# Holding the weight splits of one round in issue order, loading a quarter unit later, and moving one logits block's split

## The chip, the cores and the metric

The kernel runs on one core of a Trainium2 chip. The metric is device time in microseconds of one execution; the kernel before took 1881.35 us, the median of 3 runs (1880.4 to 1882.02).

## The reference

The computation is an attention step with 32 packed queries, a feed-forward layer with squared ReLU, and a mixture of 8 experts whose gates are balanced in 8 alternating steps over rows and columns. B = 4, H = 8, S = 576, so N = 2304 tokens of D = 512.

```python
def _moe_ref(x, w_in, w_out) -> np.ndarray:
    h = np.maximum(x @ w_in, 0.0)
    return (h * h @ w_out).astype(np.float32)
...
    logits = x @ w_gate
    logits = logits - logits.max()
    P = np.exp(logits)
    for _ in range(8):
        P /= P.sum(1, keepdims=True) + 1e-09
        P /= P.sum(0, keepdims=True) + 1e-09
        P *= N / E
    out = np.zeros((N, D), dtype=np.float32)
    for e in range(E):
        h = np.maximum(x @ w1[e], 0.0)
        ye = h @ w2[e]
        out += P[:, e:e + 1] * ye
```

## The kernel before

Every fp32 operand of a matmul is split into a hi and a lo half in float32r, and a product is three matmuls (hi·hi, hi·lo, lo·hi). The first expert layer, x @ w1, runs as seven block products by a Strassen-like scheme: w1 is taken as A11, A12, A22 and the sums S1 to S4, x as B11, B21, B22 and T1 to T4.

The tokens go through the experts in three groups. The first, 512 tokens (two halves of 256), is the "512-token round": from 426.8 to about 790 us of the span, before which the kernel does attention and the feed-forward layer, and after which the two other groups follow from kept, already split weights. The round has NQ = 32 units (a quarter of an expert's 1024 hidden columns each, some 11 us). `unit(n, ...)` issues the seven products into three PSUM banks X, Z and Y (line 679: 128x256 matmuls, six a product), the copies of partial sums (`s`, ACT, lines 740, 748, 751), the adds (VectorE: line 742 the first Y add, 755 the Z add, 758 the second Y add), and after each a ReLU into a hi half (ACT, line 686) and a lo half (VectorE, line 687) of h. Between products it issues one y unit, the matmuls of an older unit's h with w2 (line 709, 128x512). After products A12, S2, S3 and A22 it calls `hook(n, i, at)` for quarter i = 0 to 3.

A hook does the weights' work: `split_w` takes the next blocks of the table `splits` (a unit has two of w2 and four of w1). One split is a hi half on ACT (line 160), a lo half on GpSimd (line 161) and for w1 a store of both to DRAM on SP's queue. w1's block 0 also issues four sums on VectorE into one tile `wt` (lines 137 to 140), which blocks 1 and 2 are split from. When a raw tile has given its last split, `load_w` issues the next load (512 KB, ACT's queue, line 109). In this round two of every four raw tiles come from a pool `rx` whose space was used by earlier pools, `cvt` (tags cc, cr, cx) and `bdp0` of `ab` among them.

The hook then does what the table `extra` names, such as logits, and in units 2 to 7 one step of `balance`: `rows_step` (VectorE, lines 639 to 644: sums of rows rs, their reciprocal, the product P, column sums cs) or `cols_step` (a matmul on cs, line 649, and lines 651 to 653).

The order on each engine comes from a scheduler that may move instructions ahead of others. For n > 0 `extra` and the balancing stand inside `pinned()`, which makes what is issued in it come after the last instruction so far of every engine; the splits stand outside it.

`logits_split(k, ...)` splits block k of the second layer's input x2 into four tiles lx (ACT line 447, GpSimd line 448) and `logits(k, ...)` multiplies them with the gate weights (line 455), copies the result (line 458), transposes it (line 462) and copies it into P (line 463). Block 7's four tiles lie in `bdp0` and in the three tags of `cvt`; block 8's in four tiles of tag h2 in `pb`.

Of the kernel before, what the change touches and what calls it, by code (L numbers as in the profile page):

```python
# [11 lines left out]
F32R = mybir.dt.float32r  # L12
# [12 lines left out]
BT = 2 * S // 3  # L25
# [12 lines left out]
def kernel(ctx: ExitStack, tc: tile.TileContext, qT, kT, v, pT,  # L38
# [3 lines left out]
    @contextmanager  # L42
    def pinned():

        traced = nc.cur_bb.bb.instructions
        with ExitStack() as st:
            for engine in {i.engine for i in traced[-400:]}:
                st.enter_context(tc.issue_after(next(i for i in reversed(traced) if i.engine == engine)))
            yield

    def open_pool(name, **kw):
        st = ExitStack()
        return st, st.enter_context(tc.tile_pool(name=name, bufs=1, reuse_waits="tile", **kw))

    def pool(name, **kw):
        st, p = open_pool(name, **kw)
        ctx.push(st)
        return p
# [8 lines left out]
    stAB, ab = open_pool("ab", side="right")  # L67
# [26 lines left out]
    STEPS = ("A11", "S1", "S4", "S2", "S3", "A12", "A22")  # L94
    W, raw = {}, {}
    wpools = [wpa, None, None]
    state = {"load": 0, "split": 0}

    def load_w():
        k = state["load"]  # L100
        if k >= len(loads):
            return
        state["load"] += 1
        kind, src = loads[k]
        more = state.get("more")
        where = stage if more is None or (k - more[0]) % 4 >= 2 else more[1]
        t = where.tile([128, 512], I64, tag="raw", name="raw64", bufs=2) if kind == "f64" else \
            where.tile([128, 1024], F32, tag="raw", name="raw", bufs=2)
        (nc.sync if more is None else nc.scalar).dma_start(t, src)
        raw[k] = t  # L110

    def from_f64(t):

        v = t.bitcast(I32).rearrange("p (n two) -> p n two", two=2)
        high, low = v[:, :, 1].bitcast(F32), v[:, :, 0].bitcast(U32)
        a = cvt.tile([128, 512], F32, tag="cx", name="ca")
        c = cvt.tile([128, 512], I32, tag="cc", name="cc")  # L120
        r = cvt.tile([128, 512], I32, tag="cr", name="cr")
        nc.scalar.activation(a, high, AF.Copy, scale=2.0 ** -112)
        nc.vector.tensor_scalar(c, a.bitcast(I32), 3, None, op0=ALU.logical_shift_left)
        nc.scalar.activation(r, low, AF.Copy, scale=2.0 ** -29)
        nc.vector.scalar_tensor_tensor(c, a.bitcast(I32), -0x80000000, c, op0=ALU.bitwise_and, op1=ALU.bitwise_or)
        nc.gpsimd.tensor_tensor(c, c, r, op=ALU.add)
        return c.bitcast(F32)
# [16 lines left out]
    def split_w(n=1):  # L144
        for _ in range(n):
            k = state["split"]
            if k >= len(splits):
                return
            state["split"] += 1
            key, l, i = splits[k]  # L150
            part = k % 12 >= 8
            w = wpools[part].tile([128, 2, 512], F32R, tag="w", name="w", bufs=4 if part else 8)
            if loads[l][0] == "f64":
                t = from_f64(raw[l])
            elif key[0] == "w2":
                t = raw[l][:, i * 512:(i + 1) * 512]
            else:
                t = w1_blocks(raw[l], i)
            n = t.shape[1]
            nc.scalar.activation(w[:, 0, :n], t, AF.Copy)  # L160
            nc.gpsimd.tensor_tensor(w[:, 1, :n], t, w[:, 0, :n].bitcast(F32), op=ALU.subtract)  # L161
            W[key] = w
            if key[0] == "w1":
                there = kept.tile([128, 2, 512], F32R, name=f"kept_w1_{key[1]}_{i}")
                nc.sync.dma_start(there[:, :, :n].bitcast(F32), w[:, :, :n].bitcast(F32))
                KEPT[key[1], i] = there, n
            if k + 1 == len(splits) or splits[k + 1][1] != l:
                load_w()


    AT = [(ta if b < 2 else ab).tile([128, 2, 2, S], F32R, tag=f"at{b}", name=f"at{b}", bufs=1) for b in range(B)]
# [145 lines left out]
    def bank(kind):  # L317
        r = banks[kind]
        p, tag, bufs = r[turn[kind] % len(r)]
        turn[kind] += 1  # L320
        return p.tile([128, 512], F32, tag=tag, name="ps" + kind, bufs=bufs)
# [3 lines left out]
    def gslot(f, b, g):  # L325

        if f == 0:
            return b // 2, b % 2
        if f == 1:
            return ((1, 0), (0, 0))[g] if b < 2 else (3 - b, 1)  # L330
        return (1, g) if b < 2 else (0, b - 2)
# [3 lines left out]
    def g_unit(f, bp, j):  # L335

        ps = bank("h")
        w = W["win", f, j]
        st = BDP[bp]
        for i, (x, y) in enumerate(((0, 0), (0, 1), (1, 0))):  # L340
            nc.tensor.matmul(ps, st[:, x, j, :], w[:, y, :], start=(i == 0), stop=(i == 2))  # L341
        for bb in range(2):
            b = 2 * bp + bb
            if j % 2 == 0:
                side, n = gslot(f, b, j // 2)
                gt[b] = gpools[side].tile([128, 2, 512], F32R, tag=f"g{n}", name="g", bufs=2)
                G[f, b, j // 2] = gt[b]
            r = ((j % 2) ^ bb) * 64
            hi, lo = gt[b][r:r + 64, 0, :], gt[b][r:r + 64, 1, :]
            nc.scalar.activation(hi, ps[r:r + 64, :], AF.Copy)  # L350
            nc.vector.tensor_tensor(lo, ps[r:r + 64, :], hi.bitcast(F32), op=ALU.subtract)

    HT, HB1 = {}, 6
# [87 lines left out]
    def logits_split(k, places):  # L441
        p = next(q for q in (2, 1, 0) if GROUPS[q][0] <= 256 * k)
        o = 256 * k - GROUPS[p][0]
        for kd, (where, tag) in enumerate(places):
            t = where.tile([128, 2, 256], F32R, tag=tag, name="lx", bufs=HB1 if tag == "h2" else 1)
            src = X2[p][:, kd, o:o + 256]
            nc.scalar.activation(t[:, 0, :], src, AF.Copy)
            nc.gpsimd.tensor_tensor(t[:, 1, :], src, t[:, 0, :].bitcast(F32), op=ALU.subtract)
            LG[k, kd] = t
# [58 lines left out]
    stPB, pb = open_pool("pb", side="right")  # L508
# [51 lines left out]
    for i, (f, c) in enumerate(seq):  # L560
        if i < 3:
            continue
        k = c + len(THIRDS) - len(BLOCKS[f])
        last = f == NFC - 1
        if k < 2 and f > 0:
            for j in (2 * k, 2 * k + 1):
                g_unit(f, 1, j)
        if last and k == 0:
            nc.sync.dma_start(wgr, wg)
            nc.gpsimd.memset(wgs.bitcast(F32), 0.0)  # L570
            nc.scalar.activation(wgs[:, :, 0:E], wgr, AF.Copy)
            nc.vector.tensor_tensor(wgs[:, :, E:2 * E], wgr, wgs[:, :, 0:E].bitcast(F32), op=ALU.subtract)
        moe1(i, [lambda: logits_step(*MIDDLE[k])] if last and k in MIDDLE else (), 2 if i == 3 else 0)
        if last:
            logits_step(*END[k])
        if last and k == 2:
            stG.close()
            xca = pool("xca", side="left")
            T0 = {i: xca.tile([128, 4, 2, GROUPS[0][1]], F32R, tag=f"x{i}", name="xc0", bufs=1) for i in (0, 2)}
            operand(0, "B11", (T0[0][:, 0], T0[0][:, 1]), nc.gpsimd)  # L580
            operand(0, "B21", (T0[0][:, 2], T0[0][:, 3]), nc.gpsimd)
            operand(0, "B22", (T0[2][:, 0], T0[2][:, 1]), nc.gpsimd)
        if last and k == 3:
            for i in (1, 3):
                T0[i] = ta.tile([128, 4, 2, GROUPS[0][1]], F32R, tag=f"at{i // 2}", name="xc0", bufs=1)
            operand(0, "T1", (T0[1][:, 0], T0[1][:, 1]), nc.vector)
            operand(0, "T2", (T0[1][:, 2], T0[1][:, 3]), nc.vector)
        if last and k == 4:
            operand(0, "T3", (T0[2][:, 2], T0[2][:, 3]), nc.vector)
            x21, x22 = x_block(0, 1, 0), x_block(0, 1, 1)  # L590
            nc.vector.tensor_tensor(x21, x21, x22, op=ALU.subtract)
        split_w({2: 3, 3: 3, 4: 2}.get(k, 0))
        if k in (3, 4) and f + 1 < NFC:
            for j in (2 * (k - 3), 2 * (k - 3) + 1):
                g_unit(f + 1, 0, j)
    logits_split(8, ((pb, "h2"),) * 4)
    stPB.close()
    stCV.close()
# [222 lines left out]
        extra[22 + 2 * k, 3] = lambda k=k, name=name: operand(2, name, xc_tile(2, *SLOT[name]), (nc.gpsimd, nc.vector)[k % 2])  # L821

    def hook(n, i, at):
        split_w((2, 2, 1, 1)[i])
        if n == 0:
            extra.get((n, i), lambda: None)()
            return
        with pinned():
            extra.get((n, i), lambda: None)()
            if n > 2 and i != 1 or (n, i) == (2, 3):  # L830
                balance()
# [322 lines left out]
```

## Time and profile before

| what | us |
| --- | --- |
| median of 3 runs | 1881.35 |
| lowest, highest | 1880.4, 1882.02 |
| the profiled execution itself | 1880.53 |
| its span | 1878.7 |
| TensorE busy | 1854.2 |
| VectorE, GpSimd, ACT busy | 1275.1, 1047.3, 832.5 |

The profiled execution is 0.8 us below the median. PE is TensorE, DVE is VectorE, POOL is GpSimd, SP is the engine whose queue holds the stores. The page gives busy time by engine and the chain of work that ended last; windows cut the span into stages; waits say which instruction of another engine ended an engine's idle time; a timeline lists one engine's instructions in order of time.

### The profile page before, as it was taken

To read this page: it belongs to the slowest core of one execution; us is meant where nothing else is said; L and a number is where in the kernel's file an instruction comes from. 1 tells how busy PE (TensorE), PEld (TensorE's weight loads), DVE (VectorE), ACT (ScalarE), POOL (GpSimd) and SP (SyncE) were. 2 spreads that over 40 slices of the span, in tenths; PEclk is the share of its full clock that TensorE was granted. 3 is DMA by queue.
4 is the path that set the end of the run, shared out by engine and by line. 5 is a ranking of instruction groups with operands and counts; after the bars stand their busy time and mean duration, and the time that the engine had idled before them with its cause. 6 is when DMAs were issued, how large, how long until landed. Compare 5 with 4: busy or idle time off the path is not lost.

```text
span 1878.7 us, 28608 instructions
## 1 busy us (share of the span) xinstructions
PE 1854.2 (99%) x10244; PEld 1687.8 (90%) x10244; DVE 1275.1 (68%) x2095; ACT 832.5 (44%) x1557; POOL 1047.3 (56%) x655
## 2 busy tenths in 40 slices
PE   8999999999999999999999999999999999999998
PEld 7899999998888898888888888888889999999998
DVE  5767676744755556478877887788775666666665
ACT  6667554544465455444434343343334232332323
POOL 3214221436667677367877877777774444444444
PEclk9999999999999999999999999999999999999999
DMA  7402210206788877677777677676788777777874
GB/s 283 160 25 89 68 45 24 102 1 221 251 271 309 303 267 274 211 231 245 241 239 254 223 252 253 229 247 231 241 293 289 261 263 265 259 262 247 265 252 146
DMA packets 153821, 403.55 MB, mean 215 GB/s; under 512 B 14232, under 2 KB 65360, under 8 KB 153680
## 3 DMA queue, kind: packets, MB, share of 16 engines
q1 hardware_dynamic: 118928, 345.10, 54.0%
q10 hardware_dynamic: 34752, 56.63, 9.8%
q8 instruction: 81, 1.33, 0.3%
q14 instruction: 60, 0.49, 0.1%
HBM read 273.96 MB, written 127.72 MB: 214 GB/s over the span
## 4 chain that ended last, share of the span: by engine, by line
PE 93%; DVE 3%; ACT 1%; POOL 1%; DMA 1%; issue 1%; ACTq 0%; DVEq 0%; POOLq 0%
PE psc L679 35%; PE psx L1044 16%; PE psz L1044 12%; PE psy L399 11%; PE psy L709 8%; PE psh L380 6%; PE psh L341 1%; PE pp L247 1%; PE s L281 1%; POOL w L161 1%; PE s L215 0%; ACT w L160 0%; PE psy L455 0%; DVE wt L139 0%; DMA raw<-w 0%
## 5 line engine op out<-in xcount | busy, mean ns | idle before, releaser
L679 PE MATMUL psc<-xc,w 128*128 128x256 f32 (+2 forms) x4032 | 778.2, 336 | 3.0 <-ACT s L740 1.2
L679 PEld LDWEIGHTS psc<-xc,w 128*128 128x128 f32 x4032 | 666.2, 188 | 69.2 <-DVE psc L758 1.6
L1020 POOL TENSOR_TENSOR hh<-hb,hh 128x1024 fp32r<-128x1024 f32 (+1 forms) x224 | 504.4, 2256 | 372.4 <-ACT hh L1019 298.2
L1019 ACT ACTIVATE hh<-hb 128x1024 fp32r<-128x1024 f32 (+1 forms) x224 | 213.9, 955 | 448.3 <-DVE hb L1017 194.7
L1044 PE MATMUL psx<-hh,wa 128*128 128x512 f32 (+1 forms) x1536 | 352.7, 362 | 0.0
L1044 PEld LDWEIGHTS psx<-hh,wa 128*128 128x128 f32 x1536 | 278.9, 188 | 30.1 <-ACT hh L1019 0.4
L1044 PE MATMUL psz<-hh,wa 128*128 128x512 f32 (+1 forms) x1152 | 261.8, 362 | 0.3 <-issue 0.3
L1044 PEld LDWEIGHTS psz<-hh,wa 128*128 128x128 f32 x1152 | 209.1, 188 | 22.8 <-issue 0.6
L161 POOL TENSOR_TENSOR w<-raw,w 128x512 fp32r<-128x512 f32 (+1 forms) x128 | 156.6, 1237 | 124.5 <-ACT w L160 111.8
L399 PE MATMUL psy<-h,w 128*128 128x384 f32 (+1 forms) x1200 | 222.3, 330 | 0.3 <-ACT x L405 0.3
L709 PE MATMUL psy<-w,hh 128*128 128x512 f32 x768 | 202.9, 396 | 4.6 <-ACT hh L686 3.6
L399 PEld LDWEIGHTS psy<-h,w 128*128 128x128 f32 x1200 | 200.7, 188 | 0.9 <-ACT x L405 0.5
L1052 DVE TENSOR_TENSOR acc<-psx,acc 128x512 f32<-128x512 f32 (+1 forms) x248 | 151.9, 617 | 70.6 <-PE psx L1044 69.5
L1052 DVE TENSOR_TENSOR acc<-psz,acc 128x512 f32<-128x512 f32 (+1 forms) x184 | 112.6, 619 | 93.0 <-PE psz L1044 93.0
L950 DVE SCALAR_TENSOR_TENSOR hb<-psc,gate 128x512 f32<-128x512 f32 (+1 forms) x256 | 157.2, 619 | 12.2 <-PE psc L679 7.3
L709 PEld LDWEIGHTS psy<-w,hh 128*128 128x128 f32 x768 | 135.3, 189 | 29.6 <-ACT hh L686 5.3
L924 POOL TENSOR_TENSOR wa<-rb,wa 128x512 fp32r<-128x512 f32 x80 | 132.6, 1666 | 41.1 <-ACT wa L923 30.7
L1017 DVE TENSOR_TENSOR hb<-hb 128x1024 f32<-128x1024 f32 (+1 forms) x96 | 133.1, 1387 | 28.8 <-POOL hh L1020 27.9
L380 PE MATMUL psh<-at,g 128*128 128x384 f32 (+2 forms) x768 | 127.2, 304 | 0.0
L380 PEld LDWEIGHTS psh<-at,g 128*128 128x128 f32 x768 | 114.2, 189 | 1.7
L161 POOL TENSOR_TENSOR w<-cc,w 128x512 fp32r<-128x512 f32 x32 | 42.1, 1315 | 107.7 <-ACT w L160 72.5
L161 POOL TENSOR_TENSOR w<-wt,w 128x512 fp32r<-128x512 f32 x64 | 83.3, 1313 | 19.9 <-ACT w L160 15.1
(144 smaller groups left out, 1862.1 us busy)
## 6 DMA issues: line engine op xcount, KB each, us to landing
w<-kept_w SPq DMA_DIRECT2D x184, 512.0 KB, 4.4
kept_w<-wa SPq DMA_DIRECT2D x112, 512.0 KB, 4.3
wa<-kept_w SPq DMA_DIRECT2D x112, 512.0 KB, 4.5
kept_w<-w SPq DMA_DIRECT2D x96, 512.0 KB, 4.8
raw<-w ACTq DMA_DIRECT2D x60, 512.0 KB, 5.8
rb<-w ACTq DMA_DIRECT2D x64, 256.0 KB, 4.4
w<-kept_w SPq DMA_DIRECT2D x61, 256.0 KB, 4.0
raw<-win SPq DMA_DIRECT2D x16, 512.0 KB, 3.9
```

The lines of the kernel that those rows point to most:

```text
L161: nc.gpsimd.tensor_tensor(w[:, 1, :n], t, w[:, 0, :n].bitcast(F32), op=ALU.subtract)
L380: nc.tensor.matmul(ps[:, u - begin:w - begin], gw[:, x, m * 128:(m + 1) * 128], at[:, y, g, u - b * S:w - b * S], start=(i == 0), stop=(i ...
L399: nc.tensor.matmul(ps[:, :n], w[:, x, d * 128:(d + 1) * 128], h[:, y, :], start=(i == 0), stop=(i == 11))
L679: last = nc.tensor.matmul(ps[:, :N], w[:, u, o + k * 128:o + (k + 1) * 128], x[v][:, k, :], start=(start and k + u + v == 0), stop=(k == 1 ...
L709: nc.tensor.matmul(ps, h[:, x, o:o + 128], w[:, y, :], start=(n % 4 + m + x + y == 0), stop=(n % 4 == 3 and m == 1 and x == 1), skip_group ...
L924: nc.gpsimd.tensor_tensor(w[:, 1], src, w[:, 0].bitcast(F32), op=ALU.subtract)
L950: nc.vector.scalar_tensor_tensor(HB[q][m, t][:, nn, :], src, 0.0, GATE[p, g // 4][:, t * N:(t + 1) * N], op0=ALU.max, op1=ALU.mult)
L1017: nc.vector.tensor_tensor(src, src, hb[MINUS[k]], op=ALU.subtract)
L1019: nc.scalar.activation(hi, src, AF.Copy)
L1020: nc.gpsimd.tensor_tensor(lo, src, hi.bitcast(F32), op=ALU.subtract)
L1044: nc.tensor.matmul(ps, A2[q, k][:, u, nn, d * 128:(d + 1) * 128], OPS[7 * q + k][v][:, nn, :], start=(first and nn + u + v == 0), stop=(nn ...
L1052: nc.vector.tensor_tensor(a, ps, a, op=ALU.add)
```

## The change

It has three parts. In the round, the call of `split_w` moves inside `pinned()`, so that from unit 1 on a quarter's splits (ACT, GpSimd, VectorE's sums and SP's stores) come after the last instruction issued before them on each engine. The load that a finished raw tile sets off is no longer issued at once but counted in `state["due"]` and issued at the start of the next hook. And block 7's split lies in one tile of nine rows, in the space of `at3`, in place of the four tiles in `bdp0` and `cvt`; tiles that nobody uses turn the rotation of h2 so that block 8's split takes other slots. Line numbers behind the diff's places shift by up to 15 (679 becomes 691, 686 becomes 698, 687 becomes 699, 709 becomes 721, 742 becomes 754, 755 becomes 767, 758 becomes 770).

```diff
--- before.py
+++ after.py
@@ -94,7 +94,7 @@
     STEPS = ("A11", "S1", "S4", "S2", "S3", "A12", "A22")
     W, raw = {}, {}
     wpools = [wpa, None, None]
-    state = {"load": 0, "split": 0}
+    state = {"load": 0, "split": 0, "due": 0}
 
     def load_w():
         k = state["load"]
@@ -165,7 +165,14 @@
                 nc.sync.dma_start(there[:, :, :n].bitcast(F32), w[:, :, :n].bitcast(F32))
                 KEPT[key[1], i] = there, n
             if k + 1 == len(splits) or splits[k + 1][1] != l:
-                load_w()
+                state["due"] += 1
+            if "more" not in state:
+                load_due()
+
+    def load_due():
+        while state["due"]:
+            state["due"] -= 1
+            load_w()
 
 
     AT = [(ta if b < 2 else ab).tile([128, 2, 2, S], F32R, tag=f"at{b}", name=f"at{b}", bufs=1) for b in range(B)]
@@ -441,8 +448,11 @@
     def logits_split(k, places):
         p = next(q for q in (2, 1, 0) if GROUPS[q][0] <= 256 * k)
         o = 256 * k - GROUPS[p][0]
+        if k == 7:
+            whole = ab.tile([128, 9, 256], F32R, tag="at3", name="lx7", bufs=1)
         for kd, (where, tag) in enumerate(places):
-            t = where.tile([128, 2, 256], F32R, tag=tag, name="lx", bufs=HB1 if tag == "h2" else 1)
+            t = whole[:, 1 + 2 * kd:3 + 2 * kd, :] if k == 7 else \
+                where.tile([128, 2, 256], F32R, tag=tag, name="lx", bufs=HB1 if tag == "h2" else 1)
             src = X2[p][:, kd, o:o + 256]
             nc.scalar.activation(t[:, 0, :], src, AF.Copy)
             nc.gpsimd.tensor_tensor(t[:, 1, :], src, t[:, 0, :].bitcast(F32), op=ALU.subtract)
@@ -593,6 +603,8 @@
         if k in (3, 4) and f + 1 < NFC:
             for j in (2 * (k - 3), 2 * (k - 3) + 1):
                 g_unit(f + 1, 0, j)
+    for _ in range(-len(HT) % HB1):
+        pb.tile([128, 2, BT], F32R, tag="h2", name="unused", bufs=HB1)
     logits_split(8, ((pb, "h2"),) * 4)
     stPB.close()
     stCV.close()
@@ -821,11 +833,14 @@
         extra[22 + 2 * k, 3] = lambda k=k, name=name: operand(2, name, xc_tile(2, *SLOT[name]), (nc.gpsimd, nc.vector)[k % 2])
 
     def hook(n, i, at):
-        split_w((2, 2, 1, 1)[i])
         if n == 0:
+            load_due()
+            split_w((2, 2, 1, 1)[i])
             extra.get((n, i), lambda: None)()
             return
         with pinned():
+            load_due()
+            split_w((2, 2, 1, 1)[i])
             extra.get((n, i), lambda: None)()
             if n > 2 and i != 1 or (n, i) == (2, 3):
                 balance()
```

The order of TensorE in unit 0, around the logits of block 7 (lx, lx7: the split x2; psc: a product's bank; w_4777: a half of w2). Before:

```order
L679 MATMUL psc_4757<-xc0_4419,w_4246 128x256 x6
L455 MATMUL psy_4816<-lx_4698,wgs_1354 128x256 x2
L455 MATMUL psy_4816<-lx_4701,wgs_1354 128x256 x2
L455 MATMUL psy_4816<-lx_4704,wgs_1354 128x256 x2
L455 MATMUL psy_4816<-lx_4707,wgs_1354 128x256
L679 MATMUL psc_4756<-xc0_4419,w_4246 128x256 x6
L679 MATMUL psc_4757<-xc0_4229,w_4251 128x256 x6
L709 MATMUL psy_5010<-w_4777,hh_4774 128x512 x2
L709 MATMUL psy_5038<-w_4777,hh_4774 128x512 x2
L679 MATMUL psc_4756<-xc0_4229,w_4251 128x256 x6
L709 MATMUL psy_5010<-w_4777,hh_4774 128x512
L709 MATMUL psy_5038<-w_4777,hh_4774 128x512
L455 MATMUL psy_4816<-lx_4707,wgs_1354 128x256
```

Now:

```order
L691 MATMUL psc_4756<-xc0_4419,w_4246 128x256 x6
L465 MATMUL psy_4815<-lx7_4698,wgs_1354 128x256 x8
L691 MATMUL psc_4755<-xc0_4419,w_4246 128x256 x6
L472 MATMUL psy_4826<-both_1355,lgT_4824 128x8 x2
L691 MATMUL psc_4756<-xc0_4229,w_4251 128x256 x6
L721 MATMUL psy_5007<-w_4776,hh_4773 128x512 x2
L721 MATMUL psy_5035<-w_4776,hh_4773 128x512 x2
L721 MATMUL psy_5007<-w_4776,hh_4773 128x512
L721 MATMUL psy_5035<-w_4776,hh_4773 128x512
```

All eight matmuls on the split stand together, where the eighth stood behind two products and six y matmuls.

The order of ACT from the end of unit 0 into unit 1 (P: the gate copy; raw: a weight as loaded; psc_4887 and psc_4884: bank X of unit 1). Before:

```order
L686 ACTIVATE hh_4877<-psc_4756 128x256
L463 ACTIVATE P_1357<-psy_4827 128x16
L109 DMA raw_4752<-w2 128x1024
L109 DMA raw_4754<-w1 128x1024
L463 ACTIVATE P_1357<-psy_4867 128x16
L160 ACTIVATE w_4908<-raw_4752 128x512
L160 ACTIVATE w_4911<-raw_4752 128x512
L740 ACTIVATE s_4890<-psc_4887 128x256
L748 ACTIVATE s_4916<-psc_4888 128x256
```

Now:

```order
L109 DMA raw_4751<-w2 128x1024
L109 DMA raw_4753<-w1 128x1024
L698 ACTIVATE hh_4876<-psc_4755 128x256
L473 ACTIVATE P_1357<-psy_4866 128x16
L752 ACTIVATE s_4887<-psc_4884 128x256
L698 ACTIVATE hh_4902<-psc_4886 128x256
L109 DMA raw_4905<-w1 128x1024
L160 ACTIVATE w_4907<-raw_4751 128x512
L160 ACTIVATE w_4910<-raw_4751 128x512
L760 ACTIVATE s_4913<-psc_4885 128x256
```

Two loads that stood behind the gate copy stand ahead of it, and the s copy of unit 1 stands ahead of the two splits of w2 that read the first of them, not behind.

The order of VectorE in unit 3, from the lo half of h to the second Y add. Before:

```order
L687 SCALAR_TENSOR_TENSOR hh_5179<-psc_5163,hh_5179 128x256
L639 TENSOR_REDUCE rs_5196<-P_1357 128x18
L640 TENSOR_SCALAR rs_5196<-rs_5196 128x18
L641 RECIPROCAL rs_5196<-rs_5196 128x18
L137 TENSOR_TENSOR wt_5364<-raw_5147 128x256
L139 TENSOR_TENSOR wt_5364<-raw_5147 128x256
L642 TENSOR_TENSOR P_1357<-P_1357,rs_5196 128x144
L138 TENSOR_TENSOR wt_5364<-wt_5364,raw_5147 128x256
L755 TENSOR_TENSOR psc_5162<-psc_5162,s_5211 128x256
L644 TENSOR_REDUCE cs_5201<-P_1357 128x8
L140 TENSOR_TENSOR wt_5364<-raw_5147,wt_5364 128x256
L758 TENSOR_TENSOR psc_5163<-psc_5161,s_5203 128x256
```

Now:

```order
L699 SCALAR_TENSOR_TENSOR hh_5176<-psc_5160,hh_5176 128x256
L651 TENSOR_REDUCE rs_5193<-P_1357 128x18
L652 TENSOR_SCALAR rs_5193<-rs_5193 128x18
L653 RECIPROCAL rs_5193<-rs_5193 128x18
L654 TENSOR_TENSOR P_1357<-P_1357,rs_5193 128x144
L656 TENSOR_REDUCE cs_5198<-P_1357 128x8
L137 TENSOR_TENSOR wt_5219<-raw_5042 128x256
L139 TENSOR_TENSOR wt_5219<-raw_5042 128x256
L138 TENSOR_TENSOR wt_5219<-wt_5219,raw_5042 128x256
L767 TENSOR_TENSOR psc_5159<-psc_5159,s_5208 128x256
L140 TENSOR_TENSOR wt_5219<-raw_5042,wt_5219 128x256
L770 TENSOR_TENSOR psc_5160<-psc_5158,s_5200 128x256
```

The row step now stands in one piece ahead of the four sums of wt, which were mixed with it, and three of the sums stand ahead of the Z add in either order. On ACT and GpSimd the two splits of unit 3's own w2 have moved too: before they stood ahead of the unit's first s copy, now they stand behind its first hi half of h, with one split of w1 behind them.

## Rows read from the trace of the kernel before

**Rows 1.** The page: busy time of the engines, and the chain that ended last, by engine

```profile
PE 1854.2 (99%) x10244; PEld 1687.8 (90%) x10244; DVE 1275.1 (68%) x2095; ACT 832.5 (44%) x1557; POOL 1047.3 (56%) x655
...
PE 93%; DVE 3%; ACT 1%; POOL 1%; DMA 1%; issue 1%; ACTq 0%; DVEq 0%; POOLq 0%
```

**Rows 2.** Windows by stage: length, busy time (x instructions), granted clock, DMA share, GB/s

```profile
426.80:441.18 14.38, 14.13 (x93) 12.29 (x91) 4.28 (x10) 5.41 (x15) 8.39 (x9) 1.00 0.71 231
441.18:454.15 12.97, 10.62 (x63) 8.46 (x62) 8.78 (x14) 6.60 (x16) 9.28 (x9) 1.00 0.54 189
454.15:543.28 89.13, 85.25 (x525) 74.38 (x525) 62.88 (x154) 48.02 (x111) 57.07 (x47) 1.00 0.74 255
543.28:785.20 241.92, 239.66 (x1491) 213.47 (x1489) 130.73 (x264) 126.85 (x297) 168.82 (x132) 1.00 0.83 285
785.20:805.00 19.80, 19.17 (x84) 15.24 (x84) 15.62 (x23) 6.41 (x11) 1.29 (x1) 1.00 0.50 170
sum 378.20, PE 368.84 PEld 323.84 DVE 222.30 ACT 193.28 POOL 244.85; mean PE 73.77 PEld 64.77 DVE 44.46 ACT 38.66 POOL 48.97
```

**Rows 3.** TensorE's waits, 426.8 to 805 us: total us, times, longest

```profile
PE psy L709 <- ACT hh L686: 3.6, 6, 0.8
PE psy L649 <- DVE cs L644: 2.2, 4, 0.6
```

**Rows 4.** TensorE's timeline: start, us, line, operation, [idle before <-releaser]

```profile
429.00 0.99 PE L455 MATMUL psy<-lx,wgs 128*128 128x256 f32 x7
...
433.89 0.28 PE L455 MATMUL psy<-lx,wgs 128*128 128x256 f32 x1
...
473.60 0.39 PE L649 MATMUL psy<-cs,ones 128*128 128x8 f32 x2 [0.53 <-DVE cs L644]
```

**Rows 5.** ACT's timeline, unit 1

```profile
437.77 0.82 ACTq L109 DMA_DIRECT2D raw<-w  x2
...
443.09 1.15 ACT L160 ACTIVATE w<-raw 128x512 fp32r<-128x512 f32 x2 [1.62 <-DMA raw<-w]
```

**Rows 6.** VectorE's timeline, unit 1

```profile
444.40 0.95 DVE L137 TENSOR_TENSOR wt<-raw 128x256 f32<-128x256 f32 x1 [5.08 <-DMA raw<-w]
```

**Rows 7.** GpSimd's timeline, unit 0

```profile
431.78 1.45 POOL L448 TENSOR_TENSOR lx<-x,lx 128x256 fp32r<-128x256 f32 x2
```

**Rows 8.** TensorE's timeline, unit 3: its first four products

```profile
467.14 3.11 PE L679 MATMUL psc<-xc,w 128*128 128x256 f32 x24
```

**Rows 9.** VectorE's timeline, unit 3

```profile
469.81 0.42 DVE L687 SCALAR_TENSOR_TENSOR hh<-psc,hh 128x256 fp32r<-128x256 f32 x1 [0.45 <-ACT hh L686]
...
470.47 0.41 DVE L640 TENSOR_SCALAR rs<-rs 128x18 f32<-128x18 f32 x1
...
472.26 0.30 DVE L642 TENSOR_TENSOR P<-P,rs 128x144 f32<-128x144 f32 x1
...
473.47 0.41 DVE L140 TENSOR_TENSOR wt<-raw,wt 128x256 f32<-128x256 f32 x1
...
476.85 1.23 DVE L640 TENSOR_SCALAR rs<-rs 128x18 f32<-128x18 f32 x1
...
478.41 1.05 DVE L642 TENSOR_TENSOR P<-P,rs 128x144 f32<-128x144 f32 x1
```

**Rows 10.** GpSimd's timeline, unit 3

```profile
476.75 1.30 POOL L161 TENSOR_TENSOR w<-raw,w 128x512 fp32r<-128x512 f32 x1 [1.20 <-ACT w L160]
478.01 1.29 POOL L161 TENSOR_TENSOR w<-wt,w 128x512 fp32r<-128x512 f32 x1
```

**Rows 11.** Groups of VectorE and GpSimd, 426.8 to 785 us: busy us, mean ns

```profile
L139 DVE TENSOR_TENSOR wt<-raw 128x256 f32<-128x256 f32 x29 | 22.6, 781 | 0.0
...
L642 DVE TENSOR_TENSOR P<-P,rs 128x144 f32<-128x144 f32 x8 | 5.5, 688 | 0.1
L161 POOL TENSOR_TENSOR w<-raw,w 128x512 fp32r<-128x512 f32 x94 | 129.4, 1390 | 80.2 <-ACT w L160 68.8 <-DMA kept_w<-w 6.7 <-PE psc L679 4.1
```

**Rows 12.** The page's DMA issues: KB each, median us to landing

```profile
raw<-w ACTq DMA_DIRECT2D x60, 512.0 KB, 5.8
```

## The prediction

> **What bounds the kernel now.** I read the page first: TensorE is busy for 1854.2 us of a span of 1878.7 and has 93% of the chain that ended last [rows 1]. So nothing can be won except TensorE's idle time, about 24 us in all, and anything that makes TensorE wait longer is paid in full. The granted clock is 1.00 in each stretch of the round [rows 2], so no price here is one of the clock.
>
> Next the windows by stage: the round that the change touches runs from 426.8 to 805 us and holds 378.20 - 368.84 = 9.4 us of that idle time (the sum of the stretches [rows 2]). A stretch's length less TensorE's busy time says where it lies: 0.25 in unit 0, 12.97 - 10.62 = 2.35 in unit 1, 89.13 - 85.25 = 3.9 in units 2 to 7 with the balancing, 2.3 from unit 8 on (0.5 of it just ahead of 785.2) and 0.6 in the passage to the next round. Ahead of 421 us the order of every engine is unchanged, and behind the round only some loads of later weights are issued a few places apart, some 40 us ahead of their first use. So the change can win 9.4 us at most, 0.5% of the run. What a measurement of this kernel can tell from no change is about 0.2%, which is 3.8 us.
>
> Then the waits that end TensorE's idle time in the round: most are ended by ACT's evacuations of h (3.6 us in 6 waits, the longest 0.8) and VectorE's column sums of the balancing (cs: 2.2 in 4) [rows 3]. The timeline puts the four for cs, of which one stands in [rows 4], into units 3 to 5; with four of 0.3 to 0.65 for h they make up the 3.9 of units 2 to 7. Unit 1 has one wait for ACT's s copy and two for h.
>
> **Units 0 and 1: the wait for raw goes.** ACT issued the first two loads into the new raw tiles at 437.77, behind a gate copy that ends the logits of block 7, since the tiles lie on the space of that block's split x2. ACT then stood idle for the load until 443.09, with two splits of w2, which read it, next in its queue and the s copy of unit 1 behind them [rows 5], and VectorE stood 5.08 us on the same load, with the first sum of wt ahead of the Y add [rows 6]. TensorE's three waits in unit 1, 2.35 us, follow from this. In the new order the loads stand before the gate copy, and s and hh stand ahead of the first split that needs a load, so I take off all of it: **-2.35**.
>
> **Unit 0: a new wait.** Before, TensorE did seven of the eight matmuls of logits 7 at 429.00 and the eighth at 433.89, behind other work [rows 4]. Now all eight stand together ahead of the S2 product. The eighth needs the last lo half of the split x2, which stands in GpSimd's order where it stood, behind three splits from raw and one from wt: it starts at 431.78, and a pair takes 1.45, so the first of the two is done at 432.5 [rows 7]. TensorE has done seven by 429.9 and waits 2.6; the 0.25 at 430.25 lies inside that. **+2.35**: the two terms cancel.
>
> **Units 2 to 7: the balancing meets the splits.** Now each quarter unit's splits are held behind that quarter's evacuation, and the balancing steps behind these. I walk unit 3, from its first product (467.14 in the trace); in the trace the lo half of h ends 3.1 us in [rows 8, 9].
>
> What decides is what VectorE's operations on SBUF cost beside GpSimd. In the trace the scalar add on rs took 0.41 alone and 1.23 when GpSimd's split ran from 476.75 to 478.05; the product P took 0.30 alone and 1.05 when one ran from 478.01 to 479.30. Each ended within 0.2 us of that split's end [rows 9, 10]. So they waited for the running split. The sums of wt show the same: the 29 of L139 average 0.78, where 0.41 is one alone [rows 9, 11].
>
> With that cost in full: rs ends 3.4 us in, the splits of w2 run on GpSimd from 3.3 to 4.6 and to 5.9 and the next one to 7.2 (1.3 each [rows 10]). The scalar add ends at 4.6, the reciprocal at 4.9, P at 6.0, cs at 6.45. The first sum of wt waits until 7.2 and ends at 7.4; two more sums, the Z add, the fourth sum and the Y add follow at about 0.34 each, to 9.1. TensorE: four products end at 2.95 [rows 8], the first y matmuls wait 0.3 for w2's hi half and take 0.7, S4 and S3 (1.43) end at 5.4, the matmul on cs waits 1.0, four y matmuls end at 7.5, and A22, which accumulates onto what the Y add reads, waits 1.6. That is **2.9** with the rest, where before had 0.53. If instead no operation waits for GpSimd (0.41, 0.30, sums 0.41), cs is there at 4.75 and the Y add is done at 6.9, where A22 could start at 6.5: **0.7**. The same walk by the long prices gives 0.9, 2.9, 2.3, 1.05, 1.35 and 2.9 for units 2 to 7, 11.4 together; by the short ones I put 2.0 for the six. Against today's 3.9 the term lies between **-1.9 and +7.5**. In the trace about half of these operations are lengthened (a mean of 0.78 between 0.41 and some 1.2); now GpSimd's three splits stand back to back exactly where rows_step runs, which is nearer the long end, so I take two thirds of the way: **+4.4**.
>
> The Trainium skill's page "SBUF — State Buffer", section "SBUF: two separate sides", says that a VectorE operation with two SBUF inputs and a GpSimd one that reads SBUF exclude each other for a whole instruction. The trace agrees for P (1.05 beside a split, 0.30 alone). By that rule every one of them would wait, the term would be +7.5 and the time about 1889.
>
> **Units 8 to 31.** No balancing runs here. By the same walk the Z and Y adds keep 1 to 2 us ahead of the product that needs them, and the last w2 half arrives before its y matmuls. The 2.3 - 0.5 = 1.8 of this stretch may go or stay, and as many as four waits of the longest kind for h (0.8 [rows 3]) may come: -1.8 to +3, and I take **0**. The loads start a quarter unit later, 2.8 us of 11; a raw tile is then read about a unit after its issue, and a load has landed in 5.8 [rows 12], so this costs nothing; a load slower than some 10 us would be the end of that cover. The two unused h2 tiles and one tile in place of four add no work.
>
> **Sum.** 1880.53 (the profiled execution) - 2.35 + 2.35 + 4.4 + 0 = 1884.9. The median of the runs is 0.8 above the profiled one: **1885.7**, 0.23% over 1881.35.
>
> **The rivals.**
> *Faster.* VectorE's balancing and sums find gaps between GpSimd's splits. Then units 2 to 7 take their short end (-1.9), and with order on ACT the lone waits for h go as well (-1.8); if also half of the wait for the eighth logits matmul is covered because GpSimd reaches the last lo half sooner (-1.2), the time is 1881.35 - 4.9 = 1876.4. It turns on GpSimd: GpSimd has gaps (80 us of idle time ahead of its splits of raw, most of it ended by ACT's hi halves [rows 11]), and a sum that falls into such a gap costs 0.41. Against it: three of GpSimd's six splits of a unit need no sum and stand ahead of the first. It decides for faster if fewer than about one in five of these operations is lengthened. Chance 0.16.
> *No change.* The gain at units 0 and 1 and the cs waits are given back by the eighth matmul and a third of the contention: -1.9 + 0.33 x 9.4 = +1.2, so 1882.5; without any contention, but with today's lone waits, 1879.5. This also holds the case in which the held order does little because the dependencies had set it already. For it: the total at stake is small, and half the contended operations are paid now. Chance 0.40.
> *Slower*, the forecast, 1885.2 to 1892 (long end +7.5 and +3). Chance 0.44.
>
> **How the numbers follow.** Slower by over 0.2% is over 1885.1, faster is under 1877.6. The range takes in the no-change case whole, the near edge of the faster one, and the forecast up to its long end of 1889: 1877 to 1890; outside lie some 0.12 below and 0.06 above. The slower case's own range is 1885 to 1890.
>
> **What would show it.** Right: TensorE no longer waits for s at unit 1's start, and ACT's split waits for raw no more; a wait of some 2.6 us before the eighth logits matmul near 430, ended by GpSimd; in units 3, 4 and 7 waits of TensorE ended by VectorE's cs or Y add; P and the scalar add on rs near 1 us in most steps (P's mean is now 0.69 [rows 11]). Wrong: if P and the sums fall towards 0.4, the faster rival holds; if waits for cs stay and none for the Y add appears, no change; if w waits for raw in later units, my cover for the later loads was wrong.

## The result, and the profile after

The changed kernel takes 1894.55 us (median of 4 runs, 1894.45 to 1897.33) against 1881.03 for the kernel before, measured beside it: a ratio of 1.0075, 95% interval 1.0057 to 1.0092. It is slower by 13.5 us, in the direction forecast and three times as far. The profiled execution has a span of 1892.7 us, 14.0 more than before.

The page of the changed kernel, the two parts that answer to [rows 1]:

```profile
PE 1858.3 (98%) x10244; PEld 1689.8 (89%) x10244; DVE 1313.7 (69%) x2095; ACT 831.3 (44%) x1557; POOL 1052.8 (56%) x655
...
PE 91%; DVE 5%; ACT 1%; issue 1%; POOL 1%; DMA 0%; ACTq 0%; POOLq 0%; DVEq 0%
PE psc L691 35%; PE psx L1059 16%; PE psz L1059 12%; PE psy L406 11%; PE psy L721 8%; PE psh L387 6%; PE psh L348 1%; PE pp L254 1%; PE s L288 1%; DVE wt L137 1%; DVE wt L139 1%; DVE wt L138 1%; PE s L222 0%; POOL w L161 0%; PE psy L465 0%
```

TensorE is busy 4.1 us longer with the same instructions, so its idle time has grown by 9.9, not 14.0; VectorE is busy 38.6 us longer (1313.7 - 1275.1), also with the same instructions, and the sums of wt (lines 137 to 139) are now in the chain. Both need an explanation that the order of the instructions alone doesn't give.

Windows by stage, to be held against [rows 2]. The stages of before are cut here where the same work ends in the changed kernel (columns: length, busy time of TensorE, its weight loads, VectorE, ACT, GpSimd, then clock, DMA share, GB/s):

```profile
426.80:441.18 14.38, 11.90 (x74) 10.77 (x73) 3.77 (x9) 4.78 (x14) 8.27 (x8) 0.88 0.50 179
441.18:454.15 12.97, 12.97 (x81) 11.22 (x79) 7.01 (x13) 6.17 (x15) 7.41 (x7) 1.00 0.58 209
454.15:547.00 92.85, 83.15 (x514) 72.01 (x514) 70.44 (x150) 46.19 (x109) 54.87 (x45) 1.00 0.67 228
547.00:819.00 272.00, 264.34 (x1586) 231.80 (x1587) 179.35 (x290) 134.23 (x311) 179.89 (x136) 0.99 0.79 273
```

Length less TensorE's busy time: unit 0 2.48 (before 0.25), unit 1 nothing (2.35), units 2 to 7 9.7 (3.9), from unit 8 into the passage 7.7 (2.9). The waits behind this, to be held against [rows 3]:

```profile
PE psy L721 <- ACT hh L698: 8.5, 5, 2.9
PE psc L691 <- DVE psc L770: 5.2, 4, 2.1
```

TensorE's waits for cs are gone, and so are the waits for raw that ACT and VectorE had in unit 1. In their place stand h from ACT (8.5 us in 5 waits, the longest 2.9) and the second Y add, line 770 now. Where they lie, and the one of unit 0:

```profile
432.46 0.39 PE L465 MATMUL psy<-lx,wgs 128*128 128x256 f32 x1 [2.48 <-POOL lx L458]
...
476.38 0.98 PE L691 MATMUL psc<-xc,w 128*128 128x256 f32 x6 [2.09 <-DVE psc L770]
...
489.27 1.19 PE L721 MATMUL psy<-w,hh 128*128 128x512 f32 x4 [1.74 <-ACT hh L698]
...
528.19 0.98 PE L691 MATMUL psc<-xc,w 128*128 128x256 f32 x6 [2.10 <-DVE psc L770]
...
754.27 0.74 PE L721 MATMUL psy<-w,hh 128*128 128x512 f32 x2 [2.89 <-ACT hh L698]
```

Two of them are followed by a stretch at half clock. Windows of 4 us behind the wait of 2.48 and behind that of 2.89:

```profile
434.00:438.00 4.00, 4.00 (x15) 3.46 (x15) 1.28 (x3) 1.16 (x5) 1.06 (x2) 0.57 0.71 270
755.00:759.00 4.00, 3.92 (x17) 3.73 (x17) 1.71 (x6) 2.08 (x6) 2.86 (x3) 0.57 0.94 305
```

The granted clock averages 0.57 there: it is at half, 1.2 of 2.4 GHz, for 3.4 us, and gives away 4 x 0.43 = 1.7 us each time. These two make 3.4 of the 4.1 us by which TensorE is busy longer. Behind the waits of 2.09, 1.74 and 2.10 the clock stayed at 1.00.

VectorE in unit 3 and GpSimd beside it, to be held against [rows 9, 10]:

```profile
471.13 1.00 DVE L654 TENSOR_TENSOR P<-P,rs 128x144 f32<-128x144 f32 x1
...
472.52 1.05 DVE L137 TENSOR_TENSOR wt<-raw 128x256 f32<-128x256 f32 x1
473.49 1.50 DVE L139 TENSOR_TENSOR wt<-raw 128x256 f32<-128x256 f32 x1
474.91 0.41 DVE L138 TENSOR_TENSOR wt<-wt,raw 128x256 f32<-128x256 f32 x1
...
475.91 0.42 DVE L770 TENSOR_TENSOR psc<-psc,s 128x256 f32<-128x256 f32 x1
```

```profile
470.69 4.02 POOL L161 TENSOR_TENSOR w<-raw,w 128x512 fp32r<-128x512 f32 x3 [4.66 <-ACT w L160]
```

The product P and the first two sums of wt each end within 0.3 us of the end of one of the three splits that GpSimd does from 470.69 to 474.71 (4.02 us, 1.34 each): they wait for it. The third sum starts behind the splits and takes 0.41 again. The Y add ends at 476.33 (475.91 + 0.42), and the A22 product starts at 476.38.

### The profile page after: what moved, and what is told of

It is laid out like the page before. It is cut to its first block, busy times and chain, and to the rows that moved or that the text cites. A ratio compares the mean times of both kernels' runs of the same rounds, so it can differ in the third digit from the quotient of the medians.

```text
span 1892.7 us, 28655 instructions
## 1 busy us (share of the span) xinstructions
PE 1858.3 (98%) x10244; PEld 1689.8 (89%) x10244; DVE 1313.7 (69%) x2095; ACT 831.3 (44%) x1557; POOL 1052.8 (56%) x655
## 4 chain that ended last, share of the span: by engine, by line
PE 91%; DVE 5%; ACT 1%; issue 1%; POOL 1%; DMA 0%; ACTq 0%; POOLq 0%; DVEq 0%
PE psc L691 35%; PE psx L1059 16%; PE psz L1059 12%; PE psy L406 11%; PE psy L721 8%; PE psh L387 6%; PE psh L348 1%; PE pp L254 1%; PE s L288 1%; DVE wt L137 1%; DVE wt L139 1%; DVE wt L138 1%; PE s L222 0%; POOL w L161 0%; PE psy L465 0%
```

## The experiments

I held one theory against two rivals. A: the held order puts VectorE's four sums of wt ahead of the Z and Y adds, at a moment when GpSimd has a row of splits to do, and each sum waits there for a split. B: ACT's hi halves, held ahead of evacuations (ACT's copies out of PSUM, hh and s), delay these. C: the loads, issued later, make the splits late. Beside these, the new place of block 7's split was to cost one wait near 432 us. The first four kernels take the change apart.

**Place alone**, on the kernel before:

```diff
+        if k == 7:
+            whole = ab.tile([128, 9, 256], F32R, tag="at3", name="lx7", bufs=1)
...
+    for _ in range(-len(HT) % HB1):
+        pb.tile([128, 2, BT], F32R, tag="h2", name="unused", bufs=HB1)
```

> The kernel before with the new place of block 7's split and the turned h2 slots alone. TensorE's order then already has all eight matmuls on the split together. Theory A (the new place makes the eighth matmul wait, the held order makes the rest): a wait of 2.5 us ended by GpSimd near 432, the clock at half for some 3.5 us behind it (about 1.9 us), unit 1's waits of 2.35 us gone, units 2 to 31 as before: 1881 + 2.5 + 1.9 - 2.4 = 1883. Rival (the wait near 432 comes from the held order): no such wait, 1878.7.

Measured 1888.86 (1885.94 to 1890.14), ratio 1.0038 (1.0023 to 1.0053). TensorE's timeline:

```profile
432.56 0.39 PE L458 MATMUL psy<-lx,wgs 128*128 128x256 f32 x1 [2.48 <-POOL lx L451]
...
454.88 1.29 PE L684 MATMUL psc<-xc,w 128*128 128x256 f32 x6 [1.64 <-DVE psc L763]
...
643.36 1.20 PE L714 MATMUL psy<-w,hh 128*128 128x512 f32 x4 [1.78 <-ACT hh L691]
```

The wait near 432 is there, so it comes from the new place. But the gain of unit 1 did not stay. Of its waits 0.6 is left; two sums of wt meet GpSimd's splits right behind it (0.98 and 1.48 us, at 452.09 and 453.00), and the Y add at 454.88 is late by 1.64, with a second stretch of half clock behind it (clock 0.50 from 456 to 458). A wait of 1.78 at 643.36 stands where before had 0.68. By these, +2.5 for the wait near 432 and 1.7 for the clock behind it, -2.35 + 0.6 in unit 1, +1.6 and 1.7 at 454.88 and +1.1 at 643.36 make about 7. My 1883 was wrong, since it left out that the waits of the unheld order move too.

**Held order alone**, on the kernel before:

```diff
-        split_w((2, 2, 1, 1)[i])
         if n == 0:
...
         with pinned():
+            split_w((2, 2, 1, 1)[i])
```

> The kernel before with the splits held in order alone; loads at once, split in its old place. Theory A (VectorE's sums of wt, held ahead of the Z and Y adds, wait there for GpSimd's splits) and theory B (ACT's hi halves, held ahead of evacuations, delay these): units 2 to 7 idle near 9.6 us instead of 3.9 and the later units near 6.6 instead of 2.4, so 1889 to 1893. Theory C (the later loads are what makes the splits late): no more than 1882.

Measured 1902.18 (1899.32 to 1905.18), ratio 1.0111 (1.0096 to 1.0126): worse than the whole change, and beyond my numbers. TensorE's waits in the round:

```profile
PE psy L709 <- ACT hh L686: 13.2, 8, 3.8
PE psc L679 <- DVE psc L758: 4.1, 3, 1.9
PE psy L709 <- DVE acc L719: 3.4, 5, 1.1
```

C falls: each load is issued with its split, as before, and no split waits for raw that did not before. The held order alone makes the loss, and the rest of the change takes some 8 us of it back. One part of these 8 shows in the trace: a load issued at once now has its place in ACT's order too, and there it waits for GpSimd. One such load starts at 752.85, right behind a split that ends at 752.82. ACT stands idle for 2.29 us, until 753.23, with an operand's half and a hi half of h behind the load, and the wait of TensorE that follows in this unit is 3.76 (at 762.11), where the change has 2.89. The rest I did not settle.

**Deferred loads alone**, on the kernel before:

```diff
             if k + 1 == len(splits) or splits[k + 1][1] != l:
-                load_w()
+                state["due"] += 1
...
     def hook(n, i, at):
+        load_due()
         split_w((2, 2, 1, 1)[i])
```

> The kernel before with the loads issued a quarter unit later, nothing held. Theories A and B: 1881, within 2 us either way. Theory C (late loads): most of the 13.5 us, above 1888, with TensorE's waits led back to splits that wait for raw.

Measured 1884.38 (1883.4 to 1886.06), ratio 1.0019 (1.0009 to 1.0028). Units 2 to 7 have the waits of before to 0.01 us; a wait of 0.95 at 546 is new, and one of 1.83 at 691 behind a sum of 2.61 us, which ran into GpSimd's half of an operand (2.41). No wait of TensorE, ACT or VectorE for raw is new. So C has some 3 of the 13.5 us, which is beyond the 2 that I allowed. Alone the three parts cost 7.8, 21.1 and 3.3 us, together 13.5: what a part costs depends on the others.

**The last lo half on VectorE**, on the changed kernel:

```diff
-            nc.gpsimd.tensor_tensor(t[:, 1, :], ...)
+            (nc.vector if (k, kd) == (7, 3) else nc.gpsimd).tensor_tensor(t[:, 1, :], ...)
```

> The changed kernel with the last lo half of block 7's split on VectorE, which is idle then, in place of GpSimd behind four weight splits. Theory A: the wait of 2.48 us near 432 shrinks below 0.5 and the clock stays at full there, so 1894.5 - 2.2 - 1.9 = 1890.5. If the fallen clock behind that wait costs nothing, 1892.3; if the wait only moves to the next block's logits, 1894.

Measured 1895.39 (1893.88 to 1895.8), ratio 1.0074 (1.0059 to 1.0089), no gain over the change and above all three of my numbers. The wait of 2.48 is gone and so is the half clock behind it. TensorE's timeline in unit 3, and two windows, of the run's start and behind that wait:

```profile
473.94 1.36 PE L691 MATMUL psc<-xc,w 128*128 128x256 f32 x6 [2.10 <-DVE psc L770]
```

```profile
51.00:59.00 8.00, 6.57 (x24) 5.41 (x25) 7.81 (x20) 5.58 (x12) 2.77 (x3) 0.57 0.49 168
474.00:478.00 4.00, 4.00 (x17) 3.61 (x18) 3.04 (x11) 1.51 (x4) 2.99 (x3) 0.57 1.01 311
```

The same wait for the Y add that cost 2.09 in the changed kernel now costs 2.10 and is followed by half clock: 4 x 0.43 = 1.7. And this profiled execution was at half clock longer at its start (0.57 over 8 us, where the kernel before and the changed one have 0.79), ahead of all that was edited, which costs 1.7 more. 2.48 + 1.7 won, 1.7 + 1.7 lost: by these some 0.8, and the span is 0.6 shorter. So the same wait has a stretch of half clock behind it in one kernel and not in the other; what decides this no run here shows.

The second four test A, and B beside it.

**Sums late**, on the changed kernel: `wt` is made with block 1, which is issued a quarter later.

```diff
...
-        if i == 0:
+        if i == state["late"]:
...
-            split_w((2, 2, 1, 1)[i])
+            state["late"] = 1
+            split_w((2, 1, 1, 2)[i])
```

> The changed kernel with the four sums of wt issued one quarter later, behind the Z and Y adds of their unit instead of ahead of them; everything still held, the loads still late. Theory A (the sums, held ahead of the adds, wait there for GpSimd): the waits ended by the Y add, and those for h behind it, mostly go; units 2 to 31 fall from 16 us of idle time to some 4 and the fallen clock near 755 goes too, so 1894.5 - 12 - 1.7 = 1881. Theory B (ACT's hi halves ahead of evacuations): 1891 or more, since these stay where they are.

Measured 1877.08 (1874.79 to 1878.63), ratio to before 0.9974 (0.9963 to 0.9985): 17.5 us under the change, 4 under my number, and faster than the kernel before. TensorE's idle time from unit 2 into the passage is 3.4 us, where the change has 17.4 and the kernel before 6.8, so waits that were there before the change have gone too. TensorE's waits in the round, and VectorE and GpSimd in unit 3:

```profile
PE psy L465 <- POOL lx L458: 2.5, 1, 2.5
PE psy L721 <- ACT hh L698: 0.9, 3, 0.3
```

```profile
474.63 0.43 DVE L767 TENSOR_TENSOR psc<-psc,s 128x256 f32<-128x256 f32 x1
475.27 0.43 DVE L770 TENSOR_TENSOR psc<-psc,s 128x256 f32<-128x256 f32 x1 [0.21 <-PE psc L691]
...
476.54 0.41 DVE L137 TENSOR_TENSOR wt<-raw 128x256 f32<-128x256 f32 x1
476.88 0.42 DVE L139 TENSOR_TENSOR wt<-raw 128x256 f32<-128x256 f32 x1
...
477.29 0.41 DVE L138 TENSOR_TENSOR wt<-wt,raw 128x256 f32<-128x256 f32 x1
...
477.74 0.42 DVE L140 TENSOR_TENSOR wt<-raw,wt 128x256 f32<-128x256 f32 x1
```

```profile
472.77 3.84 POOL L161 TENSOR_TENSOR w<-raw,w 128x512 fp32r<-128x512 f32 x3 [2.34 <-ACT w L160]
```

The sums stand behind both adds, and behind GpSimd's three splits as well: its next split reads wt, so it has to stand still until the sums are done, and here they take 0.42 or less each. The groups of the sums in the changed kernel and in this one:

```profile
L139 DVE TENSOR_TENSOR wt<-raw 128x256 f32<-128x256 f32 x29 | 32.8, 1132 | 0.0
L138 DVE TENSOR_TENSOR wt<-wt,raw 128x256 f32<-128x256 f32 x29 | 29.1, 1005 | 0.0
L140 DVE TENSOR_TENSOR wt<-raw,wt 128x256 f32<-128x256 f32 x29 | 27.0, 932 | 0.5
L137 DVE TENSOR_TENSOR wt<-raw 128x256 f32<-128x256 f32 x29 | 26.3, 906 | 4.4 <-POOL w L161 4.4
```

```profile
L137 DVE TENSOR_TENSOR wt<-raw 128x256 f32<-128x256 f32 x29 | 14.4, 495 | 0.0
L139 DVE TENSOR_TENSOR wt<-raw 128x256 f32<-128x256 f32 x29 | 14.3, 492 | 0.0
...
L140 DVE TENSOR_TENSOR wt<-raw,wt 128x256 f32<-128x256 f32 x29 | 12.3, 424 | 0.8
L138 DVE TENSOR_TENSOR wt<-wt,raw 128x256 f32<-128x256 f32 x29 | 12.1, 416 | 0.0
```

115.2 us against 53.1, and none of it in the way of an add. Before the sums took 77.1, so they are 38.1 of the 38.6 us by which VectorE is busier in the change. This run alone doesn't part A from B, since the hi halves of the two blocks that are split from wt moved a quarter later with the sums.

**No sums**, on the changed kernel:

```diff
-        if i == 0:
-            t = wpools[2].tile([128, 1024], F32, tag="wt", name="wt", bufs=1)
...
-        return (r[:, 0:512], sums["t"][:, 0:512], sums["t"][:, 512:1024], a22)[i]
+        return (r[:, 0:512], r[:, 0:512], r[:, 512:1024], a22)[i]
```

> The changed kernel without the sums of wt: blocks 1 and 2 of w1 are split from the raw tile's first and second half, so the products S1 to S4 use other numbers. ACT's and GpSimd's splits are as many, as long and in the same order. Theory A: as with the sums issued late or better, 1878 to 1882. Theory B: 1891 or more.

Measured 1874.71 (1874.09 to 1876.91), ratio 0.9968 (0.9955 to 0.9981). As many splits in the same order, ACT's hi halves ahead of the same evacuations as in the change, and the waits go: the sums are the cause, and B falls as a cause of its own. It is only some 2 us under the sums late, so these cost little where they stand now.

In the change a sum does reach TensorE by way of B at times. ACT's hi half of a block from wt stands ahead of evacuations and waits for the third sum itself:

```profile
707.33 0.63 ACT L160 ACTIVATE w<-wt 128x512 fp32r<-128x512 f32 x1 [3.29 <-DVE wt L138]
```

```profile
708.29 0.98 PE L691 MATMUL psc<-xc,w 128*128 128x256 f32 x6 [1.04 <-ACT s L752]
```

The copy s that TensorE waits for there stands right behind this hi half, at 707.87. Ahead of the wait of 2.89 the same order costs only 0.23: the Z add has ended at 753.63, and ACT starts on h at 753.86.

**Lo halves of the weights zero**, on the changed kernel:

```diff
-            nc.gpsimd.tensor_tensor(w[:, 1, :n], t, ...)
+            if "more" in state:
+                nc.gpsimd.memset(w[:, 1, :n].bitcast(F32), 0.0)
+            else:
+                nc.gpsimd.tensor_tensor(w[:, 1, :n], t, ...)
```

> The changed kernel with the round's lo halves of the weights set to zero by GpSimd instead of being subtracted, so GpSimd neither reads nor stays busy long; the sums stand where the change put them. If the price of theory A is the meeting with GpSimd, the sums take 0.41 each and 1881 or less comes out, with the wait near 432 gone as well: 1877 to 1881. If the sums cost by their number alone, at 0.41 each, a third or more of the idle time stays and it is 1885 or more.

Measured 1872.28 (1871.56 to 1873.44), ratio 0.9953 (0.9938 to 0.9968). The sums stand ahead of the adds as in the changed kernel, and TensorE has no wait above 0.6 us in the round: not their place alone but their meeting with GpSimd is the price. The wait near 432 is gone as well, since GpSimd's splits ahead of the last lo half are short here, so the time is to be held against that of both edits below (1872.94), not of the sums late. GpSimd's memset of 128x512 takes 0.53, where a split takes 1.3, and it reads nothing; which of the two counts, this run doesn't part. Three of the four in this run, the fourth averaging 0.68:

```profile
L140 DVE TENSOR_TENSOR wt<-raw,wt 128x256 f32<-128x256 f32 x29 | 12.2, 421 | 0.7
L139 DVE TENSOR_TENSOR wt<-raw 128x256 f32<-128x256 f32 x29 | 12.1, 417 | 0.0
L138 DVE TENSOR_TENSOR wt<-wt,raw 128x256 f32<-128x256 f32 x29 | 12.0, 415 | 0.0
```

**Both edits**, on the changed kernel: the sums late, as above, and

```diff
-            nc.gpsimd.tensor_tensor(t[:, 1, :], ...)
+            (nc.vector if (k, kd) == (7, 3) else nc.gpsimd).tensor_tensor(t[:, 1, :], ...)
```

> The sums late, and the last lo half of block 7's split on VectorE. By theory A the two add: 1881 - 2.5 - 1.7 = 1877, faster than before by 0.2%. If idle time and fallen clock only move to other places, as after the second alone, no gain over the sums late by themselves.

Measured 1872.94 (1872.3 to 1873.77), ratio 0.9956 (0.9941 to 0.9971): 8 us faster than before, 22 faster than the change. All four of this group came out 3 to 5 us under my numbers for A. Here the lo half brings 4.1 at the median, and 4.1 between the two profiled spans too: 2.0 of TensorE's idle time and 2.1 of its busy time. With the sums late alone the half clock behind the wait of 2.48 lasts about twice as long as in the change, which is 3.4 us of full clock in place of 1.7:

```profile
432.00:440.00 8.00, 7.13 (x28) 6.37 (x29) 2.03 (x5) 1.64 (x5) 3.48 (x5) 0.57 0.64 250
```

That isn't so in each of its runs: of the eight, four took 1874.79 to 1876.28 at a mean clock of 0.998 or 0.999, and four, the profiled one among them, 1877.88 to 1878.63 at 0.996. The same edit brought nothing while other long waits stood behind it.

The last three ask which parts of the change this needs.

**Sums late on the kernel before**, with nothing held:

```diff
-        if i == 0:
+        if i == state["late"]:
...
-        split_w((2, 2, 1, 1)[i])
+        state["late"] = int(n > 0)
+        split_w((2, 1, 1, 2)[i] if n else (2, 2, 1, 1)[i])
         if n == 0:
```

> The kernel before, with the sums of wt issued a quarter later but nothing held: the scheduler may still bring them forward, and in unit 3 three of the four stand ahead of the second Y add. Theory A: the sums meet GpSimd as before or somewhat less, 1879 to 1883. If issuing them late is enough without holding: 1877 or less.

Measured 1882.88 (1882.09 to 1884.87), ratio 1.0012 (1.0003 to 1.0021). The scheduler brings the sums forward again, their means stay near those of the kernel before (0.78 for line 137, which had 0.70), and waits for the Y add come (4.7 us in 5). Late issue needs the holding.

**Loads at once**, on both edits:

```diff
-                state["due"] += 1
-            if "more" not in state:
-                load_due()
+                load_w()
```

> The sums late and the last lo half on VectorE, but each load issued at once, as before the change. Theory A gives the deferred loads no part: 1873, within 2 us. If the later loads are what keeps the held order clear of waits: 1876 or more, with waits for ACT's or GpSimd's splits.

Measured 1874.62 (1873.79 to 1876.18), ratio 0.9965 (0.9953 to 0.9978). No wait of TensorE in the round is above 0.6 us, and none is for a split; the deferred loads bring 1.7 at most, and the runs of the two kernels lie that near together that I don't call it shown.

**Old place**, on the sums late: block 7's split back in `bdp0` and `cvt`, all of it on GpSimd.

```diff
-            whole = ab.tile([128, 9, 256], F32R, tag="at3", name="lx7", bufs=1)
...
-            t = whole[:, 1 + 2 * kd:3 + 2 * kd, :] if k == 7 else \
-                where.tile([128, 2, 256], F32R, tag=tag, ...)
+            t = where.tile([128, 2, 256], F32R, tag=tag, ...)
...
-    for _ in range(-len(HT) % HB1):
-        pb.tile([128, 2, BT], F32R, tag="h2", name="unused", bufs=HB1)
```

> The sums late and held, loads deferred, but block 7's split in its old place, so the two first loads wait for the gate copy again and the eighth matmul is apart from the other seven. Theory A: no wait of 2.48 near 432 and no fallen clock there, up to 2.4 us of waits for raw in unit 1: 1873.5 to 1876. If the new place is needed for the gain: 1877 or more.

Measured 1873.42 (1873.36 to 1874.43), ratio 0.996 (0.9946 to 0.9975). Unit 1's waits, which the new place was to end, come to 0.21 us: the held order already puts the s copies ahead of the splits that wait for raw. So the new place isn't needed, and moving it costs the wait of 2.48 unless the lo half is moved as well.

## Why the prediction was wrong, point by point

- **What bounds the kernel**: right that TensorE does, wrong that only its idle time counts. Of the 14.0 us, 9.9 are TensorE idle and 4.1 are TensorE busy longer, 3.4 of these by half clock.
- **Unit 1, -2.35, and unit 0, +2.35**: right, 2.35 gone and a wait of 2.48 come, at the place and by the engine named (2.48 - 0.25 = +2.2).
- **"No price here is one of the clock"**: the first step that failed, a term put at nothing that measured 3.4. I read it from a kernel whose longest wait in the round was 0.97. The wait that I forecast at 2.6 came at 2.48 with half clock behind it, and one of 2.89 in the later units, which I had not forecast, had it too: 2 x 1.7 = 3.4.
- **Units 2 to 7, +4.4 between -1.9 and +7.5**: 9.7 - 3.9 = +5.8, inside and somewhat under-sized. In unit 3 the walk had the Y add done 9.1 us in; it was done at 9.05 (476.33, with the first product at 467.28). It had A22 wait 1.6 and cs 1.0: A22 waited 2.09 and cs not at all, because the scalar add on rs slipped in before GpSimd's first split (0.18 us). That number is near its time alone, 0.16 to 0.18; the 0.41 that I took for it is already a lengthened one, since it ends with a split of GpSimd (470.47 + 0.41 against 469.56 + 1.29, in the trace of the kernel before). My sign for the balancing itself did not come: I wanted P and the scalar add near 1 us in most steps, and the mean of P fell from 0.69 to 0.55, of the scalar add from 0.66 to 0.61. It is the sums that pay: their four means, between 0.50 and 0.78 before, lie between 0.91 and 1.13.
- **Units 8 to 31, 0**: the second step that failed, and the larger. With the passage it measured +4.8, beyond its own upper end of 3. I let the Z and Y adds keep 1 to 2 us in hand by a walk in which GpSimd has only splits to do. At 747.77 it does half of a later group's operand first (2.40), then three splits (4.29), and VectorE's sums stand in front of the adds all that time:

```profile
748.34 2.12 DVE L137 TENSOR_TENSOR wt<-raw 128x256 f32<-128x256 f32 x1
750.38 1.50 DVE L139 TENSOR_TENSOR wt<-raw 128x256 f32<-128x256 f32 x1
751.81 1.48 DVE L138 TENSOR_TENSOR wt<-wt,raw 128x256 f32<-128x256 f32 x1
753.21 0.42 DVE L767 TENSOR_TENSOR psc<-psc,s 128x256 f32<-128x256 f32 x1
```

```profile
747.77 2.40 POOL L422 TENSOR_TENSOR xc<-x,xc 128x1024 fp32r<-128x1024 f32 x1 [1.76 <-ACT xc L421]
750.12 4.29 POOL L161 TENSOR_TENSOR w<-raw,w 128x512 fp32r<-128x512 f32 x3
```

Three sums take 5.1 us in place of 1.2, and y's h is late by 2.89, where the kernel before has 0.82 at this place. The three waits next in size lie behind an operand's half too: 1.04 at 708.29 and 0.85 at 609.18 behind one on GpSimd (701.74 and 603.21), 1.28 at 623.60 behind one that VectorE does itself, between the sums and the adds (620.75). I had priced contention by the operations' present mean (0.78 for line 139), which rose to 1.13, and had not gone through the units with an operand's half in them.
- **Sum**: -0.1 + 5.8 + 4.8 + 3.4 = 13.9 of 14.0, against my +4.4. That it comes out so near is in part luck: 0.7 more of busy time and 0.6 less of idle time elsewhere cancel.
- **The range** ended at 1890, though the sum's own upper ends came to 1892; with the two clock drops they would have been 1895.
- **The Trainium skill's rule** ("SBUF — State Buffer", section "SBUF: two separate sides": a VectorE operation with two SBUF inputs and a GpSimd one that reads SBUF exclude each other for a whole instruction) put units 2 to 7 at their long end, 7.5. The single operations bear it out: the sum at 748.34 ends 0.3 us behind GpSimd's 2.40. The term as a whole doesn't: 5.8 lies about midway between my 4.4 and that end. The time that I gave by the rule, 1889, left units 8 to 31 at nothing as well.
- **Rivals**: that VectorE's operations find gaps between the splits is what happens once the sums stand where GpSimd waits for them; in the change as made they did not.

## What to carry to other kernels

Where VectorE makes an operand that GpSimd reads next, put the making right where GpSimd must wait for it: there the two hardly meet (0.42 to 0.50 a sum on average, in place of 0.91 to 1.13), and here that turned a loss of 13.5 us into a gain of 4, or 8 with one more edit. An order written out by hand has to be walked for every kind of unit, the ones with extra work on the shared engine first, and a long wait that the walk leaves may have to be charged for the clock too (the tally stands below). A part that brings nothing alone may bring its full price once the longer waits behind it are gone.

## What the runs showed of the hardware that I had not expected

In the round, over the traces of all thirteen kernels, TensorE's clock fell to half (0.5) behind each of the seven single waits of 2.48 us or more, and behind three of the fifteen between 1.64 and 2.10 us: 1.64 with the place alone, 1.91 with the held order alone, 2.10 with the last lo half on VectorE. The stream was otherwise dense. The stretch at half clock lasted 3.4 us, which gives away 1.7 us of full clock, and about twice that in two kernels (the sums late, no sums). Waits of the same length had it behind them or not, and what decides that is not shown.

A sum of 128x256 on VectorE took 0.41 to 0.43 alone, and up to 2.13 beside GpSimd (2.61 with deferred loads alone). With several GpSimd operations queued in a row, each of three sums in a row lost time to one of them (2.12, 1.50 and 1.48 us).
